# Window attention on one core: softmax tiles off ScalarE with one squaring instead of two, and a part of them finished by GpSimd alone

## The chip, the core and the metric

The kernel runs on one core of a Trainium2 chip. The core has five engines that run side by side: TensorE (PE in the profile, with its weight loads as PEld), ScalarE (ACT), VectorE (DVE), GpSimd (POOL) and SyncE (SP, which here issues transfers). Matmuls write to PSUM, eight banks of 512 float32 columns in each of 128 partitions; everything else is held in SBUF. The metric is the device time of one launch in microseconds. A run of the kernel before is one of 1052.92, 1053.43 and 1056.92 us; the median is 1053.43 us.

## The reference, cut to what matters

The input is an image of 224 x 224 tokens with 96 channels. The channels are split in two halves of 48. On the first half attention runs inside horizontal strips of 8 x 224 tokens, on the second half inside vertical strips of 224 x 8 tokens; there are 28 strips of each kind, and each strip has 1792 tokens.

```python
qkv = einsum('bhwc,cd->bhwd', x, wqkv)            # 96 -> 288, bfloat16
q, k, v = qkv[..., :96], qkv[..., 96:192], qkv[..., 192:]
scale = 48 ** -0.5
# for each of 28 horizontal strips (channels 0..47) and 28 vertical ones (channels 48..95):
a = softmax(q_strip @ k_strip.T * scale, axis=-1)  # 1792 x 1792
o_strip = a @ v_strip
out = concat(o_horizontal, o_vertical) @ wo        # 96 -> 96
```

The heavy part is the softmax: 56 matrices of 1792 x 1792 exponentials.

## The kernel before, in words

**Pairs and tiles.** Two strips are worked on together as a pair, one in the upper and one in the lower half of the partitions where that is possible. There are 28 pairs (P = 0 to 27), horizontal ones first (0 to 13), vertical ones after (14 to 27). A pair's queries are cut into four chunks of 512, 512, 512 and 256 columns, its keys into 14 blocks of 128. A tile of scores is 128 keys by 512 queries for both strips of the pair, so 128 partitions x 1024 columns in two PSUM banks (in the last chunk two key blocks of 256 queries each). A pair has 49 tiles, the kernel 1372.

**A tile's way.** Scores come from four matmuls (eight in the last chunk) of K against Q. They are in units in which 128 is a factor of two of the exponential. Then the tile is turned into exponentials in bfloat16, in one of `NPT` buffers called `PT` in SBUF. Last, two matmuls per key block multiply it with V and add it up in a PSUM bank (`pv_fn`, L692); a column of ones in V gives the softmax's denominator. When a chunk's tiles are all added up, DVE copies the bank to `OT_sb` (L1151), the output projection runs (L528, L563), and DVE divides by the denominator. For vertical strips the result is added to that of the horizontal ones, either on DVE (L590) or, after a DVE step into `tmp` (L577), on POOL (L581), and written out in pieces of 24 KB.

**Two kinds of tile.** The exponentials are made in two ways, and a table says for each pair and chunk how many tiles go the second way.

- On ScalarE (1128 tiles, kind "A"): one ACTIVATE with Exp over 128 x 1024, from PSUM into `PT` (L884). It takes no bias; its scale is ln2/128.
- Off ScalarE (244 tiles, kind "P"): the scores are computed with one more row, so that a constant of 17920 = 140 x 128 is added to them, which puts a float32 score's exponent at a fixed place: its upper 16 bits are the score cut down to a multiple of 128, its lower 16 bits the rest. PE computes the tile once into PSUM banks 6 and 7 ("s1", L679). DVE reads the lower halves, scales and shifts them and writes float32 into a buffer `qb` (called p1, L1174). POOL squares `qb` in place (L1100) and squares it again into `PT` as float16 (L1101). PE computes the same tile a second time ("s2", L679 too). DVE adds the upper halves, a constant and `PT`, and writes the sum as the 16 bits of the bfloat16 exponential into `PT` (called f, L1184).

The PSUM banks are shared out: 0 to 3 are two sets for ScalarE's tiles, 4 and 5 take the sums over V, and 4 to 7 are a ring for all else, where the pair 6 and 7 serves the tiles off ScalarE and can be a third set for ScalarE.

**What sets the order.** The program is planned when it is built. A planner (class `Sched` and the functions `step_pe`, `step_dve`, `step_pool`) goes through the work with fixed durations and latencies for each operation (constants at the file's head) and picks for each engine what comes next; the result is one straight list per engine. The table `HOW` has a row for each pair: three digits, how many tiles of each of the first three chunks go off ScalarE; a number that shapes when the next pair's projections come; and four groups of digits, which are the planner's thresholds in each chunk. Engines wait for each other by semaphores that count finished instructions; `settle` leaves out a wait that is already implied by another. On POOL every operation on a tile off ScalarE waits for the one before it on the same tile by POOL's own semaphore. POOL takes from its queue the piece of the earliest tile that is ready.

**Buffers.** A tile holds one of the 18 `PT` buffers from its first step to its product with V, and a tile off ScalarE holds one of the 5 `qb` buffers from p1 until POOL's last step.

The lines that the change touches are L17 to L68 (constants and `HOW`), L279 and L280 (constants of the extra row), L308 and L884 (the two kinds of Exp), L555 to L590 (the projection of the vertical strips), L1096 to L1110 (POOL's steps), L1149 (the copy's planned duration), L1173 to L1187 (p1 and f) and L1252 (the order of waits).

Of the kernel before, what the change touches and what calls it, by code (L numbers as in the profile page):

```python
# [24 lines left out]
SW_AB, SW_BA = SWT["AB"], SWT["BA"]  # L25
D_ACT, P_ACT, M_ACT, SEMA = 0.904, 0.9155, 1.0175, 0.053
D_MM, L_MM, L_PV, L_FILL = 0.216, 0.465, 0.44, 0.215
W_PE, W_FIN = 0.021, 0.08
SEMD, SEMP, SELF, SEMX = 0.15, 0.10, 0.19, 0.05
D_P1, D_SQ, D_ADD = 1.135, 1.9, 0.0019  # L30

# [8 lines left out]
HOW = [  # L40
    ("222", 4, "47621910043 47621610043 48111500102 48111500052"),
    ("433", 8, "31911900232 31911900133 31921900333 34921900333"),
    ("343", 12, "34922910333 21211710344 25211710344 25211710341"),
    ("234", 0, "25211710141 38512811234 38512811203 38911811203"),
    ("253", 8, "38912811203 22842702142 20913800234 38522510103"),
    ("131", 4, "38532510103 41242400243 29341900013 29641900113"),
    ("424", 6, "29641900141 29643900104 35141900263 35143700263"),
    ("332", 5, "35143710213 31831600124 31831600024 25711910144"),
    ("333", 12, "39912600343 39912600344 39912700244 56931812314"),
    ("344", 1, "36941812314 36911812312 22941910281 22941910171"),  # L50
    ("322", 12, "54342701072 4a631600103 4a532600102 4a542600202"),
    ("432", 9, "44542600202 44442600303 54442600203 44941700233"),
    ("435", 6, "54941700233 56513710273 33923700372 53913700372"),
    ("125", 6, "20411310241 20411510241 20411510243 36413510243"),
    ("332", 9, "5a121712204 5a121712004 5a121700004 55841800091"),
    ("332", 11, "55841800191 55841801394 55841801294 55841701294"),
    ("233", 12, "34222711191 28133400114 28233800112 28233800114"),
    ("243", 9, "28933800114 28932800194 58932802294 58932802194"),
    ("422", 9, "58942802394 42642700090 23341711232 23443711232"),
    ("233", 11, "23443711232 25441711234 25441711244 25441711244"),  # L60
    ("334", 3, "25441711204 25341711234 25341710232 25343710231"),
    ("333", 7, "2a343910234 56812810121 49431900323 34641710054"),
    ("233", 3, "34641710254 26921901034 26941901094 26941901034"),
    ("224", 3, "26931901034 29911901014 37121810224 33121810324"),
    ("333", 1, "33141810324 30131810124 30131800124 30131800124"),
    ("343", 7, "50131810124 50131610224 50111610224 26431810222"),
    ("233", 4, "24421810222 24421500222 24921501022 39632900141"),
    ("333", 7, "55542710102 25542700102 30132711054 33531400391"),  # L68
]
# [91 lines left out]
def bass_standalone__window_attn_cswin__vision_kernel(  # L161
# [27 lines left out]
    with es:  # L189
# [13 lines left out]
        one_sb = sb("one_sb", [1, 8], BF16)  # L203
        scr = sb("scr", [128, 8], FP32)
        warm = sb("warm", [128, 512], BF16)
        xs_sb = sb("xs_sb", [C, 2, 4], BF16)
# [71 lines left out]

        KC = [4.8125 / 128.0, 21.0]  # L279
        QC = [0.0, 32.0]  # L280

# [133 lines left out]
        def prep_fills(P):  # L415
# [3 lines left out]
            for kind, L in (("k", K), ("q", Q)):  # L419
                for c in range(NCH):  # L420
# [14 lines left out]
                    if kind == "k":  # L435
                        def d(e, bk, c=c, q0=q0, qs=qs):
                            return e.tensor_scalar(KT_sb[b][:, q0:q0 + qs], bk[:, 0:qs], alpha, None,  # L437
                                                   ALU.mult, ALU.add, accum_out=ksum[b][:, c:c + 1])
                        chain = [(0.07 + qs * 0.001026, d, [], [("KT", b, c), ("ksum", b, c)], None)]
                        rd = ["w0z", "w"]  # L440
                        needs = [("X", P)] if P else []
                        if P >= 2:
                            needs = needs + [("PV", P - 2)]
                        L.append(fill("B", 0.216 * qs / 512, pe_fn,
                                      rd + [("xT", b, 0), ("xT", b, 1)], chain, needs, ("K", P, c)))
                    else:
                        def d(e, bk, q0=q0, qs=qs):
                            return e.tensor_copy(QT_sb[b][:, q0:q0 + qs], bk[:, 0:qs])  # L448
# [3 lines left out]
                        L.append(fill("B", 0.216 * qs / 512, pe_fn,  # L452
                                      [("xT", b, 0), ("xT", b, 1), ("wqz", ph, b), ("wqc", ph, b),
                                       ("wq", ph, b, 0), ("wq", ph, b, 1)],
                                      [(0.07 + qs * 0.001026, d, [], [("QT", b, c)], da)],
                                      [("QB", P)], ("Q", P, c)))

# [9 lines left out]
            QB = fill("B", 0.36, pe_fn, [("wqT", ph)] + [("ksum", b, c) for c in range(NCH)],  # L467
                      [(0.08, d, [("wqz", ph, b)], [("wqc", ph, b)], None)],
                      [("K", P, c) for c in range(NCH)] + [("wqT", ph)], ("QB", P))
            for k0 in range(0, 2 * NKT, VS):  # L470
# [12 lines left out]
                def d(e, bk, k0=k0, n=n):  # L483
# [3 lines left out]
                V.append(fill("B", 0.033 * n, pe_fn, ["w"] + [("xT", b, w) for w in ws],  # L487
                              [(0.065 + n * 0.05, d, ["vones"], [("V", b, k0)], None)],
                              [("X", P)] if P else [], ("V", P, k0)))
# [21 lines left out]
        def fin_fills(P, fs):  # L511
# [98 lines left out]
        def dve_commit(item, t):  # L610
# [7 lines left out]
            after = 0.07 if k == 0 and f["gives"][0] == "fin" else 0.0  # L618
            S.commit("dve", t, st[0], st[0] + SEMD + after, lambda e, fn=st[1], bk=bk: fn(e, bk),
# [256 lines left out]
        def issue_qka(t, s):  # L876
# [7 lines left out]
            S.commit("act", 0.0, D_ACT, None, lambda e, s=s, slot=slot: e.activation(  # L884
                PT[slot][:], ps[:, 512 * SETS[s]:512 * SETS[s] + 1024], ACTF.Exp, scale=LN2 / 128.0),
                set_keys(s), pt_keys(slot), fresh=pt_keys(slot))
# [208 lines left out]
        def mids(tl):  # L1095
# [3 lines left out]
            qk, yk = [("q", i), "pser"], pt_keys(tl["slot"])  # L1099
            return [("pool", D_SQ, lambda e: e.tensor_tensor(q, q, q, ALU.mult), qk, [("q", i)]),  # L1100
                    ("pool", D_SQ, lambda e: e.tensor_tensor(y, q, q, ALU.mult), qk, yk)]  # L1101

        def next_mid(tl):
# [21 lines left out]
        def step_dve():  # L1125
# [20 lines left out]
            if what == "ot":  # L1146
                P, c = it["pc"]
                q0, qs = CH_Q0[c], CH_SIZES[c]
                d = 0.07 + qs * 0.001026  # L1149
                pb = pv_bank[it["pc"]]  # L1150
# [21 lines left out]
            elif what == "p1":  # L1172
                tl = it["t"]  # L1173
                S.commit("dve", t, D_P1, D_P1 + SEMD, lambda e: e.tensor_scalar(  # L1174
                    qb[tl["qb"]][:], half(U16, 0), QS * 2.0 ** -16, QS * QH, ALU.mult, ALU.add),
# [5 lines left out]
            elif what == "f":  # L1181
                tl = it["t"]
                ptk = pt_keys(tl["slot"])
                S.commit("dve", t, D_P1, D_P1 + SEMD, lambda e: e.scalar_tensor_tensor(  # L1184
                    PT[tl["slot"]][:].bitcast(U16), half(BF16, 1), 128.0 * (126.0 - SOFF + QC0),
                    PT[tl["slot"]][:].bitcast(FP16), ALU.add, ALU.add),
# [48 lines left out]
        def settle():  # L1235
# [88 lines left out]
```

## Time and profile before

| | |
|---|---|
| median of 3 runs | 1053.43 us (1052.92 to 1056.92) |
| the profiled execution | 1052.86 us, of which the profile's span is 1051.1 us |
| granted TensorE clock | 0.999 |
| ScalarE busy | 1040.3 us, 99% of the span |
| TensorE busy | 1029.0 us, 98% |
| GpSimd busy | 970.6 us, 92% |
| VectorE busy | 957.3 us, 91% |

How to read it. Busy is the time in which at least one instruction of the engine was running. A group of instructions is one source line, one engine and one form; after it stand the count, the busy time, the mean duration of one, and how long the engine stood idle just before such instructions. Successive ScalarE instructions overlap in the records (1128 of them with a mean of 1084 ns take 1036.0 us, not 1222.8), so the mean of one is longer than the time from start to start, and the time from start to start is what counts in a sum. The same holds, with a smaller overlap, for DVE and POOL. PE's busy time is modelled and is no proof that PE works at its best. The chain of work is followed back from the last instruction to what released it, step by step.

### The profile page before, as it was taken

The page shows a single profiled execution, that of the slowest core. Times are in us where ns is not written, and L with a number is a line of the kernel's source. Part 1 is how long each engine was busy: PE and PEld are TensorE (multiplying, and loading weights), DVE is VectorE, ACT ScalarE, POOL GpSimd, SP SyncE. Part 2 cuts the span into 40 slices and gives each one's busy share as a digit, 9 for nine tenths or more (in the row PEclk, how much of TensorE's full clock was granted, in tenths as well). Part 3 has the DMA queues.
Part 4 walks back from the last instruction along what each step waited for, and adds up shares of the span by engine and source line. Part 5 has one row for each costly group of instructions (what it writes and reads, how often), then busy time and mean ns, then how long its engine had stood idle before and what let it go on. Part 6 is the DMA issues. An engine that isn't in the chain of part 4 may idle for free.

```text
span 1051.1 us, 32414 instructions
## 1 busy us (share of the span) xinstructions
PE 1029.0 (98%) x14143; PEld 421.9 (40%) x14143; DVE 957.3 (91%) x1536; ACT 1040.3 (99%) x1139; POOL 970.6 (92%) x564
## 2 busy tenths in 40 slices
PE   8999999999999999999999999999999999999997
PEld 4433444444344344434434434434343343444333
DVE  7999999989989998999998899988999999999897
ACT  8999999999999999999999999999999999999997
POOL 6999899889989997998999999999999999999995
PEclk9999999999999999999999999999999999999999
DMA  4212113212220321111012212222213221321111
GB/s 101 64 42 63 30 48 63 54 32 56 64 55 11 76 41 46 42 37 37 2 36 46 43 39 56 52 36 49 51 23 55 56 50 23 55 55 24 24 21 34
DMA packets 162880, 47.12 MB, mean 45 GB/s; under 512 B 155895, under 2 KB 162711, under 8 KB 162738
## 3 DMA queue, kind: packets, MB, share of 16 engines
q1 hardware_dynamic: 161618, 44.57, 20.2%
q8 instruction: 110, 1.80, 0.7%
q10 hardware_dynamic: 1120, 0.49, 0.2%
q14 instruction: 32, 0.26, 0.1%
HBM read 10.60 MB, written 19.28 MB: 28 GB/s over the span
## 4 chain that ended last, share of the span: by engine, by line
ACT 96%; PE 2%; DVE 1%; issue 0%; DVEq 0%
ACT PT L884 96%; PE ps L666 1%; PE ps L692 1%; PE ps L343 0%; DVE PT L1184 0%; DVE qb L1174 0%; ACT xT_sb L743 0%; PE ps L679 0%; DVE out_all L590 0%; PE ps L432 0%; DVE QT_sb L448 0%; DVE OT_sb L1151 0%; PE ps L727 0%; PE ps L528 0%; PE ps L479 0%
## 5 line engine op out<-in xcount | busy, mean ns | idle before, releaser
L884 ACT ACTIVATE PT<-ps 128x1024 bf16<-128x1024 f32 x1128 | 1036.0, 1084 | 1.4 <-PE ps L666 1.2
L1100 POOL TENSOR_TENSOR qb<-qb 128x1024 f32<-128x1024 f32 x244 | 462.3, 1895 | 38.5 <-DVE qb L1174 36.6
L1101 POOL TENSOR_TENSOR PT<-qb 128x1024 f16<-128x1024 f32 x244 | 462.3, 1895 | 17.6
L666 PE MATMUL ps<-QT_sb,KT_sb 49*64 49x512 bf16 (+1 forms) x5296 | 462.9, 364 | 14.5 <-ACT PT L884 3.0
L692 PE MATMUL ps<-PT,V_sb 128*49 128x512 bf16 (+1 forms) x3136 | 464.5, 361 | 0.2 <-ACT PT L884 0.2
L1184 DVE SCALAR_TENSOR_TENSOR PT<-ps,PT 128x1024 uint16<-128x1024 bf16 x244 | 298.4, 1223 | 37.1 <-PE ps L679 27.9
L1174 DVE TENSOR_SCALAR qb<-ps 128x1024 f32<-128x1024 uint16 x244 | 298.0, 1221 | 19.4 <-PE ps L679 17.5
L666 PEld LDWEIGHTS ps<-QT_sb,KT_sb 49*64 49x64 bf16 x5296 | 134.4, 103 | 333.9 <-ACT PT L884 305.9
L692 PEld LDWEIGHTS ps<-PT,V_sb 128*49 128x49 bf16 x3136 | 137.4, 103 | 186.8 <-issue 153.3
L679 PE MATMUL ps<-QT_sb,KT_sb 50*64 50x512 bf16 x1952 | 194.0, 387 | 1.9 <-DVE PT L1184 0.3
L1151 DVE CAST OT_sb<-ps 113x512 bf16<-113x512 f32 x112 | 69.4, 620 | 8.8 <-PE ps L692 8.0
L679 PEld LDWEIGHTS ps<-QT_sb,KT_sb 50*64 50x64 bf16 x1952 | 55.6, 103 | 50.1 <-DVE qb L1174 11.9
L448 DVE CAST QT_sb<-ps 128x512 bf16<-128x512 f32 (+1 forms) x111 | 68.1, 616 | 5.6 <-PE ps L432 5.2
L437 DVE TENSOR_SCALAR_CACHE_REDUCE KT_sb<-ps 128x512 bf16<-128x512 f32 x108 | 66.0, 615 | 0.6 <-PE ps L432 0.4
L581 POOL TENSOR_TENSOR out_all<-tmp,Ph_sb 128x480 bf16<-128x480 f32 (+1 forms) x49 | 51.2, 1049 | 8.3 <-DVE tmp L577 7.9
L486 DVE CAST V_sb<-ps 128x480 bf16<-128x480 f32 (+1 forms) x84 | 52.1, 621 | 4.1 <-PE ps L479 3.4
L543 DVE TENSOR_TENSOR Ph_sb<-ps,rc 128x480 bf16<-128x480 f32 (+1 forms) x84 | 52.2, 622 | 2.5
L479 PEld LDWEIGHTS ps<-w_sb,xT_sb 96*64 96x64 bf16 x1568 | 36.0, 112 | 11.7 <-issue 5.8
L432 PE MATMUL ps<-xT_sb,wq_sb 97*64 97x512 bf16 x224 | 40.4, 360 | 0.0
L590 DVE SCALAR_TENSOR_TENSOR out_all<-ps,rc,Ph_sb 128x96 bf16<-128x96 f32 x160 | 39.2, 310 | 1.2
L432 PE MATMUL ps<-xT_sb,w_sb 97*64 97x512 bf16 x224 | 40.0, 359 | 0.0
L479 PE MATMUL ps<-w_sb,xT_sb 96*64 96x48 bf16 x1568 | 38.9, 190 | 0.0
(59 smaller groups left out, 274.5 us busy)
## 6 DMA issues: line engine op xcount, KB each, us to landing
cols_dram<-in_x_dram SPq DMA_DIRECT2D x28, 336.0 KB
out_dram<-out_all SPq DMA_DIRECT2D x386, 24.0 KB, 1.9
xT_sb<-cols_dram SPq DMA_TRANSPOSE x28, 4.5
xT_sb<-in_x_dram SPq DMA_TRANSPOSE x26, 4.2
xT_sb<-ones_dram SPq DMA_DIRECT2D x26, 7.0 KB
Ph_sb<-in_x_dram SPq DMA_DIRECT2D x2, 168.0 KB, 3.5
Ph_sb<-in_x_dram ACTq DMA_DIRECT2D x2, 168.0 KB, 3.7
out_dram<-out_all ACTq DMA_DIRECT2D x6, 24.0 KB, 1.9
```

The costliest lines, as they stand in the source:

```text
L432: ins = e.matmul(bk[64 * w:64 * w + 64, 0:qs], lhsT=lw, rhs=x_of(kind, w, q0, qs), start=True, stop=True)
L448: return e.tensor_copy(QT_sb[b][:, q0:q0 + qs], bk[:, 0:qs])
L479: ins = e.matmul(bk[64 * h:64 * h + 64, j * C2:(j + 1) * C2], lhsT=xT_sb[b][0:C, w, t0:t0 + 64], rhs=w_sb[0:C, wblk(P, "v"), 0:C2], start= ...
L666: ins = e.matmul(bank(SETS[s] + w)[64 * kh:64 * kh + 64, i * t["qs"]:(i + 1) * t["qs"]], lhsT=KT_sb[b][64 * w:64 * w + CA, kt * 128 + 64 * ...
L679: ins = e.matmul(bank(PB0 + w)[64 * kh:64 * kh + 64, 0:512], lhsT=KT_sb[b][64 * w:64 * w + nr, kt * 128 + 64 * kh:kt * 128 + 64 * kh + 64] ...
L692: ins = e.matmul(bank(pb)[64 * w:64 * w + CA, 0:t["qs"]], lhsT=V_sb[b][:, w, kt, :], rhs=PT[slot][:, ca:ca + t["qs"]], start=st and i == 0 ...
L884: S.commit("act", 0.0, D_ACT, None, lambda e, s=s, slot=slot: e.activation(PT[slot][:], ps[:, 512 * SETS[s]:512 * SETS[s] + 1024], ACTF.Ex ...
L1100: return [("pool", D_SQ, lambda e: e.tensor_tensor(q, q, q, ALU.mult), qk, [("q", i)]), ("pool", D_SQ, lambda e: e.tensor_tensor(y, q, q, ...
L1101: ("pool", D_SQ, lambda e: e.tensor_tensor(y, q, q, ALU.mult), qk, yk)]
L1151: S.commit("dve", t, d, d + SEMD, lambda e: e.tensor_copy(ot_dst(P, q0, qs), ot_src(P, pb, qs)), [("bank", pb)], [("OT", P % 2, c)], tag=( ...
L1174: S.commit("dve", t, D_P1, D_P1 + SEMD, lambda e: e.tensor_scalar(qb[tl["qb"]][:], half(U16, 0), QS * 2.0 ** -16, QS * QH, ALU.mult, ALU.add),
L1184: S.commit("dve", t, D_P1, D_P1 + SEMD, lambda e: e.scalar_tensor_tensor(PT[tl["slot"]][:].bitcast(U16), half(BF16, 1), 128.0 * (126.0 - S ...
```

## The change

- A tile off ScalarE needs one squaring instead of two. DVE's p1 scales the lower halves with other constants, POOL squares `qb` straight into `PT`, and f adds another constant.
- 275 tiles instead of 244 go off ScalarE; 1097 instead of 1128 stay on it.
- 118 of the 275 are "whole": p1 is a plain copy of the scores, float32 from PSUM to `qb`. POOL then does four steps alone: it scales and shifts the lower halves of `qb` into `PT` (float16), squares `PT` in place, scales and shifts it back into the lower halves of `qb` as 16-bit whole numbers, and converts `qb` to the 16 bits of the bfloat16 exponential in `PT`. Such a tile needs no second pass of scores and no f. The planner makes a tile whole when fewer tile steps are queued for POOL than a new, twelfth digit of `HOW` says. The other 157 go the way of before with one squaring less.
- The constants of the extra row change (21.75 and 31 for 21 and 32), so the added constant is no longer a multiple of 128. To give the same factor, ScalarE's Exp gets a bias: `up`, a [128, 1] operand in SBUF that DVE sets once at the start.
- `PT` has 16 buffers instead of 18, `qb` 6 instead of 5.
- In the last pair the projection comes in groups of 4 key blocks instead of 2, and all but the last group may be added on POOL; 60 additions are put on POOL instead of 49.
- `HOW` is another table, and several planned durations differ. Among waits of one DVE instruction, one for PE is considered first when waits that are implied are left out.

```diff
-QK, QH, QC0 = 0.00302015814, 3.83652076, 0.346271089
-QS = (128.0 * QK) ** 0.25
-SOFF = 140.0
+PA, PB, PS = 0.65763628, 0.33718946, 1.00172476
+QL, QQ = 128.0 * PA / PS, 128.0 * PB / PS
+QS, QH = QQ ** 0.5, 0.5 * QL / QQ
+SOFF = 580.0 * 31.0 / 128.0
-NPT = 18
-NQB = 5
+NPT = 16
+NQB = 6
-D_P1, D_SQ, D_ADD = 1.135, 1.9, 0.0019
+D_P1, D_SQ, D_ADD = 1.14, 1.852, 0.0019
+D_TS = 1.05
 HOW = [
-    ("222", 4, "47621910043 47621610043 48111500102 48111500052"),
+    ("211", 7, "217126001431 217126001434 386325000832 461239000223"),
...
-        KC = [4.8125 / 128.0, 21.0]
-        QC = [0.0, 32.0]
+        KC = [4.8125 / 128.0, 21.75]
+        QC = [0.0, 31.0]
...
-        now("act", ["scr"], ["scr2"], lambda e: e.activation(scr[:], scr[:], ACTF.Exp), dur=1.4)
+        dve_now(["up"], lambda e: e.memset(up[:], (SOFF - 127.0) * LN2 - math.log(PS)), 0.08)
+        now("act", ["scr", "up"], ["scr2"], lambda e: e.activation(scr[:], scr[:], ACTF.Exp, bias=up[:, 0:1]), dur=1.4)
...
+                        late = P == NP - 1 and k0 + n == NKT
-                        if P < NP - 1:
+                        if not late:
...
             S.commit("act", 0.0, D_ACT, None, lambda e, s=s, slot=slot: e.activation(
-                PT[slot][:], ps[:, 512 * SETS[s]:512 * SETS[s] + 1024], ACTF.Exp, scale=LN2 / 128.0),
+                PT[slot][:], ps[:, 512 * SETS[s]:512 * SETS[s] + 1024], ACTF.Exp, bias=up[:, 0:1], scale=LN2 / 128.0),
...
-                    for need, f in fin_fills(P, 2 if P == NP - 1 else FS):
+                    for need, f in fin_fills(P, 4 if P == NP - 1 else FS):
...
             qk, yk = [("q", i), "pser"], pt_keys(tl["slot"])
-            return [("pool", D_SQ, lambda e: e.tensor_tensor(q, q, q, ALU.mult), qk, [("q", i)]),
-                    ("pool", D_SQ, lambda e: e.tensor_tensor(y, q, q, ALU.mult), qk, yk)]
+            if not tl["whole"]:
+                return [("pool", D_SQ, lambda e: e.tensor_tensor(y, q, q, ALU.mult), qk, yk)]
+            lo = q.bitcast(U16).rearrange("p (n t) -> p n t", t=2)[:, :, 0]
+            bits = PT[tl["slot"]][:].bitcast(U16)
+            return [("pool", D_TS, lambda e: e.tensor_scalar(y, lo, 2.0 ** -16, QH, ALU.mult, ALU.add), qk, yk),
+                    ("pool", D_SQ, lambda e: e.tensor_tensor(y, y, y, ALU.mult), yk + ["pser"], yk),
+                    ("pool", D_TS, lambda e: e.tensor_scalar(lo, y, 512.0 * QQ, -512.0 * QQ * QH * QH, ALU.mult, ALU.add), yk + ["pser"], [("q", i)]),
+                    ("pool", D_TS, lambda e: e.tensor_scalar(bits, q, 1.0, 0.0, ALU.mult, ALU.add), qk, yk)]
...
                 qb_free.append(tl["qb"])
+                if tl["whole"]:
+                    pv_ready[(tl["P"], tl["c"])].append((tl, tl["slot"]))
+                    return
...
-                S.commit("dve", t, D_P1, D_P1 + SEMD, lambda e: e.tensor_scalar(
+                tl["whole"] = sum(m["what"] == "mid" for m in pool_q) < how()[11]
+                S.commit("dve", t, D_P1, D_P1 + SEMD, lambda e: e.tensor_copy(
+                    qb[tl["qb"]][:], ps[:, PB0 * 512:(PB0 + 2) * 512]) if tl["whole"] else e.tensor_scalar(
                     qb[tl["qb"]][:], half(U16, 0), QS * 2.0 ** -16, QS * QH, ALU.mult, ALU.add),
...
-                    PT[tl["slot"]][:].bitcast(U16), half(BF16, 1), 128.0 * (126.0 - SOFF + QC0),
+                    PT[tl["slot"]][:].bitcast(U16), half(BF16, 1), -QQ * QH * QH,
                     PT[tl["slot"]][:].bitcast(FP16), ALU.add, ALU.add),
...
-                        for s, v in sorted((x for x in waits if x[1]), key=lambda x: (-S.done[x], x)):
+                        for s, v in sorted((x for x in waits if x[1]), key=lambda x: (not (k == "dve" and x[0] == "pe"), -S.done[x], x)):
```

More of the change, by code (lines that the diff above doesn't have):

```diff
@@ L1 @@
+import math
 from contextlib import ExitStack
@@ L49 @@
[L49 to L64, printed above, removed]
@@ new lines @@
+    ("523", 12, "392317001614 5a8225000402 488329000443 264418102934"),
+    ("444", 10, "264419102934 264419102934 264419100934 264419101933"),
+    ("334", 4, "264319101933 267319001933 367319002933 364429002933"),
+    ("234", 10, "321429002933 321429002934 321129002934 587416000033"),
+    ("333", 12, "248128100543 411438002134 4a2419113401 564417102341"),
+    ("464", 0, "564417102343 325338113240 325338113244 383128101811"),
+    ("312", 10, "349128101811 349128101812 341228101812 355128103524"),
@@ new lines @@
+    ("343", 8, "355128103522 215438100222 215428100222 2a5428100224"),
+    ("353", 7, "219138001434 279138001431 453427100024 453437000024"),
+    ("323", 12, "453437000004 354417120014 354417123014 3a4427123010"),
+    ("444", 4, "3a4427123012 244118102010 557319012933 5a8317120012"),
+    ("424", 4, "5a8317122032 5a8317022332 5a8317122332 5a8317122331"),
+    ("335", 9, "5a8317122321 4a8317122424 4a8327022424 581427101532"),
+    ("413", 10, "582227101531 299116102414 484427010830 284427010830"),
@@ new lines @@
+    ("433", 6, "382327002044 382127002842 592426111342 292426101342"),
+    ("333", 11, "296419101342 286419101342 316429101123 316439101133"),
+    ("334", 8, "341417123821 341417122821 341427122021 373429100712"),
+    ("444", 4, "576417121542 5a6417021543 5a6417002543 5a6417002243"),
+    ("323", 6, "5a6336122322 5a6336122322 4a6326122320 495225112221"),
+    ("423", 12, "495325012221 229428102632 229428102631 5a6426100122"),
+    ("434", 1, "5a6429103122 577336020343 577336020341 547336020343"),
@@ L438, in d @@
                                                    ALU.mult, ALU.add, accum_out=ksum[b][:, c:c + 1])
-                        chain = [(0.07 + qs * 0.001026, d, [], [("KT", b, c), ("ksum", b, c)], None)]
+                        chain = [(0.08 + qs * 0.001026, d, [], [("KT", b, c), ("ksum", b, c)], None)]
                         rd = ["w0z", "w"]
@@ L466, in d @@
                                        mybir.AxisListType.X, ALU.add)
-            QB = fill("B", 0.36, pe_fn, [("wqT", ph)] + [("ksum", b, c) for c in range(NCH)],
+            QB = fill("B", 0.43, pe_fn, [("wqT", ph)] + [("ksum", b, c) for c in range(NCH)],
                       [(0.08, d, [("wqz", ph, b)], [("wqc", ph, b)], None)],
@@ L487, in prep_fills @@
                 V.append(fill("B", 0.033 * n, pe_fn, ["w"] + [("xT", b, w) for w in ws],
-                              [(0.065 + n * 0.05, d, ["vones"], [("V", b, k0)], None)],
+                              [(0.075 + n * 0.05, d, ["vones"], [("V", b, k0)], None)],
                               [("X", P)] if P else [], ("V", P, k0)))
@@ L617, in dve_commit @@
                 more = [("tmp", st[6]["ti"][0])]
-            after = 0.07 if k == 0 and f["gives"][0] == "fin" else 0.0
+            after = -0.06 if k == 0 and f["gives"][0] == "fin" else 0.0
             S.commit("dve", t, st[0], st[0] + SEMD + after, lambda e, fn=st[1], bk=bk: fn(e, bk),
```

28 lines of the change are left out of this document (12 added, 16 removed).

## The prediction

> **What bounds the kernel now.** I read the page first (busy time, the chain that ended last, the costliest groups), then the chain in order of time, then POOL's timeline, its groups by shape and the load by stretches of time.
>
> ```profile
> span 1051.1 us, 32414 instructions
> PE 1029.0 (98%) x14143; PEld 421.9 (40%) x14143; DVE 957.3 (91%) x1536; ACT 1040.3 (99%) x1139; POOL 970.6 (92%) x564
> ...
> ACT 96%; PE 2%; DVE 1%; issue 0%; DVEq 0%
> ...
> L884 ACT ACTIVATE PT<-ps 128x1024 bf16<-128x1024 f32 x1128 | 1036.0, 1084 | 1.4 <-PE ps L666 1.2
> L1100 POOL TENSOR_TENSOR qb<-qb 128x1024 f32<-128x1024 f32 x244 | 462.3, 1895 | 38.5 <-DVE qb L1174 36.6
> L1101 POOL TENSOR_TENSOR PT<-qb 128x1024 f16<-128x1024 f32 x244 | 462.3, 1895 | 17.6
> ...
> L1184 DVE SCALAR_TENSOR_TENSOR PT<-ps,PT 128x1024 uint16<-128x1024 bf16 x244 | 298.4, 1223 | 37.1 <-PE ps L679 27.9
> L1174 DVE TENSOR_SCALAR qb<-ps 128x1024 f32<-128x1024 uint16 x244 | 298.0, 1221 | 19.4 <-PE ps L679 17.5
> ...
> L679 PE MATMUL ps<-QT_sb,KT_sb 50*64 50x512 bf16 x1952 | 194.0, 387 | 1.9 <-DVE PT L1184 0.3
> ...
> L581 POOL TENSOR_TENSOR out_all<-tmp,Ph_sb 128x480 bf16<-128x480 f32 (+1 forms) x49 | 51.2, 1049 | 8.3 <-DVE tmp L577 7.9
> ```
>
> The chain is 96% the Exp of L884, and that group stood idle for 1.4 us in all: ScalarE is the bound from its first tile to its last. The chain in order of time shows the pace and both ends:
>
> ```profile
> 9.14 58.88 ACT PT L884 x64
> ...
> 213.31 604.34 ACT PT L884 x658
> ...
> 1045.38 0.42 PE ps L692 x4
> ```
>
> 658 tiles take 604.34 us, 0.9185 us from start to start. Of the span, 9.1 us lie before the first tile, 1036 are tiles (1128 x 0.9185), some 6 us from 1045.38 on are the last tile's product with V, the projection and the write out. The profiled execution took 1052.86 us, 1.76 above the span, and 0.57 below the median of 1053.43.
>
> **The change part by part.**
>
> *Fewer tiles on ScalarE.* 1097 instead of 1128: 31 x 0.9185 = 28.5 us off the bound, if nothing else ends later. That is the gain to be had; the other parts decide whether it is kept.
>
> *POOL's load.* POOL is next to look at, because it takes on work of a new kind. Its rows by time and by shape:
>
> ```profile
> 14.07 1.89 POOL L1100 TENSOR_TENSOR qb<-qb 128x1024 f32<-128x1024 f32 x1 [3.82 <-DVE qb L1174]
> ...
> 503.43 1.90 POOL L1101 TENSOR_TENSOR PT<-qb 128x1024 f16<-128x1024 f32 x1
> 505.28 1.89 POOL L1100 TENSOR_TENSOR qb<-qb 128x1024 f32<-128x1024 f32 x1
> 507.25 1.89 POOL L1101 TENSOR_TENSOR PT<-qb 128x1024 f16<-128x1024 f32 x1
> ...
> 1037.34 1.89 POOL L1101 TENSOR_TENSOR PT<-qb 128x1024 f16<-128x1024 f32 x1
> ```
>
> ```profile
> L324 POOL COPY w_sb<-wst 96x192 bf16<-96x192 bf16 x1 | 0.3, 341 | 2.0 <-DMA wst<-in_wqkv_dram 2.0
> L316 POOL COPY wq_sb<-wst 96x96 bf16<-96x96 bf16 x4 | 1.1, 263 | 0.2
> L335 POOL MEMSET wqT<- 128x192 bf16 x2 | 0.5, 262 | 0.1
> L332 POOL MEMSET woh<- 128x97 bf16 x1 | 0.2, 188 | 0.1
> ```
>
> A squaring followed by work of another tile takes 1.85 us from start to start (503.43 to 505.28); followed by the next step of its own tile 1.97 (505.28 to 507.25), so a wait on POOL's own step costs 0.12. Before, POOL worked from 14.07 to 1039.23. Now the sum:
> - Squarings: 157 + 118 = 275 instead of 488, at 1.85: 509 us instead of 903. That the operands are float16 in 118 of them has no row; float16 out costs what float32 out costs (both 1895 ns), so I take the same.
> - New steps with one input (L1110, L1112, L1113 of the changed kernel): 3 x 118 = 354. None is in this trace. From below: the memsets' slope is (262 - 188) / 95 = 0.78 ns a column, which gives 188 + 927 x 0.78 = 911 ns for 1024 columns. From above: the two-input squaring, 1895 ns. Nearest is the copy, one input and one output: (341 - 263) / 96 = 0.81 ns a column, 341 + 832 x 0.81 = 1015 ns. I take 1.02: 361 us.
> - Additions: 60 instead of 49 at 1.05 (51.2 / 49): 63 us instead of 51.
> - Own waits: in the program's order 328 steps follow a step of their own tile directly, before 225: 39 us instead of 27.
>
> The total is 972 us instead of 981, in a span shorter by 28.5: 25 us spare of about 997. So POOL nearly fills its time, and the halves differ. Additions exist only for the vertical pairs:
>
> ```profile
> 20.00:540.00 520.00, 514.81 (x7088) 210.72 (x7084) 479.52 (x704) 519.88 (x567) 477.64 (x255) 1.00 0.20 47
> 540.00:1040.00 500.00, 489.88 (x6744) 198.27 (x6744) 457.90 (x774) 499.94 (x546) 481.13 (x280) 1.00 0.21 41
> ```
>
> (columns: stretch, its length, busy us of PE, PEld, DVE, ACT and POOL with counts, clock, transfer share, GB/s). In pairs 14 to 27 of the changed program stand 545 tiles on ScalarE, 500.6 us, and for POOL 141 squarings (260.9), 156 one-input steps (159.1), 60 additions (63.0) and 142 own waits (17.0): 500.0 us. In pairs 0 to 13 it is 507.0 against 472.2. So in the second half POOL has no time to spare and ScalarE will wait for it now and then: through `PT` buffers that come free late, since a chunk's sum waits for its last tile. I add 4 us for that; it is what 156 steps at 1.045 instead of 1.02 would cost. The bounds are 0, as in the trace (1.4 us idle), and, at the two-input price, 354 x 0.88 - 25 = 287 us.
>
> *DVE.* p1 275 times, f 157 times: 432 x 1.222 = 528 us instead of 596; the whole tiles' plain copy is taken at p1's price, same columns, same place read. 11 more additions move to `tmp` and POOL, and DVE's own final steps become fewer. DVE falls to some 890 us of 1023; nothing is late through it.
>
> *PE.* 275 + 157 = 432 passes of L679 instead of 488, 56 x 4 matmuls at 0.099 us (194.0 / 1952) = 22 us less, and 31 tiles of L666 less. PE's cover gets better, not worse. The clock is 1.00 in both stretches above, and PE stays about as full.
>
> *The bias.* Each of the 1097 Exp now reads `up`. Its setting is one DVE memset during the start, before ScalarE's wait for the first transposes; it costs nothing. Reading it has no row on ScalarE. Nearest are DVE's evacuations with and without a [128, 1] operand:
>
> ```profile
> L448 DVE CAST QT_sb<-ps 128x512 bf16<-128x512 f32 x83 | 56.7, 684 | 5.6 <-PE ps L432 5.2
> L448 DVE CAST QT_sb<-ps 128x256 bf16<-128x256 f32 x28 | 11.6, 414 | 0.0
> L760 DVE TENSOR_SCALAR KT_sb<-ps,kb_sb 128x512 bf16<-128x512 f32 x2 | 1.4, 748 | 1.0 <-PE ps L432 1.0
> L760 DVE TENSOR_SCALAR KT_sb<-ps,kb_sb 128x256 bf16<-128x256 f32 x1 | 0.5, 476 | 0.0
> ```
>
> With the operand one instruction is 62 ns longer at 256 columns (476 against 414) and 64 at 512. That is the mean of one, not the time from start to start. On ScalarE one instruction shows 1084 ns and the next starts after 918, so 166 ns of each lie under its neighbour, and a fetch of 62 ns has room there: the operand is constant, and the tile after next stands ready (1.4 us idle in 1128). I take 0, with 0.062 as the other end; that end is a rival below, because it would turn the sign. A gain is excluded: nothing is taken away from the instruction.
>
> *Buffers, queues, the end.* Two `PT` buffers fewer are weighed against a shorter hold: a tile with one squaring gives its `PT` up about 1.97 us sooner, 157 times; a whole one holds it about as long as before, 5.3 us of POOL steps (3 x 1.02 + 1.85 + 3 x 0.12) against 3.85 for two squarings and 1.22 for f. One more `qb` covers the whole tile's four steps. The rest of the price is in the 4 us. Transfers out stay 392; four of the last go from ACT's to SP's queue. SP issued 19 in 13.25 us at the end, 0.7 each:
>
> ```profile
> 1035.73 13.25 SPq L269 DMA_DIRECT2D out_dram<-out_all  x19
> 1044.97 4.33 ACTq L269 DMA_DIRECT2D out_dram<-out_all  x6
> ```
>
> Four more are 2.8 us at worst, nothing if they are issued before the last chunk is done, as the coarser groups of the last pair (4 blocks) make likely; no Exp stands behind those on ACT. I take 0. The changed order of DVE's waits takes no wait away; 0, bounded by DVE's idle time of 9%.
>
> *Sum.* 1052.86 - 28.5 + 4 = 1028.4 for an execution like the profiled one; with 0.57 for the median 1028.9. I say 1028.
>
> **The rivals.**
>
> *The bias is paid in full (slower).* If a fetch of 62 ns lies between two Exp, as the DVE rows would have it, ScalarE's pace is 0.980: 1028 + 1097 x 0.062 = 1096 us. The point from which it decides is 28.5 / 1097 = 0.026 us a tile. For it speaks that both widths give the same addition on DVE, so it is a fixed cost of the operand; against it the overlap of 166 ns. The Trainium skill (ScalarE: Activation LUTs, What ACT_TABLE_LOAD costs) states about 93 ns for each [128, 1] operand of an ACTIVATE; by that the sum would be 1028 + 1097 x 0.093 = 1130 us, an estimate from that page. No run so far shows an ACTIVATE with such an operand, so the trace neither agrees nor differs.
>
> *POOL becomes the bound (late, or slower).* Each 0.1 us on a one-input step adds 35 us to POOL. Up to 1.09 us (1.02 + 25 / 354) the whole still fits; at 1.17 the gain is gone; at 1.25 the time is about 972 + 81 + 26 (its start and the end after it) + 2 = 1081 us. What could do it: the lower halves are read and written two bytes of every four, and types are converted, which the copy's row does not show. In the mild case the second half's 156 steps set it, from 1024.4: 1034 is reached at 1.02 + 9.6 / 156 = 1.08, and 1048 at 1.17.
>
> *The change does nothing for the bound.* If the wait for POOL's longer tiles kept ScalarE from 28 us in all, the time would stay at 1053. No wait in the trace is near that size: all of ScalarE's idle time was 1.4 us.
>
> **How the numbers follow.** About 0.5% (5 us) is what a measurement of this kernel can tell from no change. ScalarE stays the bound and POOL just keeps up (1018 to 1034): 0.67. POOL late by some 6 to 20 us (1034 to 1048): 0.13. Below 1018: 0.01, only if ScalarE's pace itself gets better with less work on PE. No change: 0.02. POOL decidedly the bound (over 1059): 0.05. The bias paid (1075 to 1130): 0.12. So faster 0.81, same 0.02, slower 0.17. The range 1018 to 1047 is that of the first two cases, 0.80; the likeliest one's own is 1018 to 1034.
>
> **What would show it.** In the changed kernel's page: the Exp group x1097 with about 1007 us busy, 0.918 from start to start, and a few us of idle time before it; a start to start near 0.98 or 1.01 proves the bias. POOL's three one-input groups with a mean near 1.02 to 1.06; over 1.1 POOL is late, and then waits by PE for `PT` written on POOL appear and ScalarE's idle time grows, most of all after 540 us. L1107 and L1111 at 1.85 to 1.9. The chain still over 95% Exp. DVE near 890 us busy.

## The result, and the profile after

The changed kernel takes 1125.89 us (median of 4 runs, 1121.34 to 1129.87) against 1053.22 us for the kernel before on the same chip (4 runs): a ratio of 1.068, 95% interval 1.0626 to 1.0734. It is 6.8% slower. The forecast of 1028 us had the wrong sign. What came is the first rival, the bias paid in full.

The page of the changed kernel (profiled execution 1123.16 us; span, busy time, chain by engine, costliest groups):

```profile
span 1121.3 us, 31675 instructions
PE 1023.4 (91%) x13792; PEld 393.7 (35%) x13792; DVE 913.7 (81%) x1441; ACT 1106.7 (99%) x1108; POOL 985.8 (88%) x716
...
ACT 98%; PE 1%; DVE 0%; issue 0%; DVEq 0%
...
L890 ACT ACTIVATE PT<-ps,up 128x1024 bf16<-128x1024 f32 x1097 | 1102.3, 1356 | 2.5 <-PE ps L672 2.5
...
L1107 POOL TENSOR_TENSOR PT<-qb 128x1024 f16<-128x1024 f32 x157 | 294.0, 1893 | 4.8 <-DVE qb L1191 4.7
...
L1111 POOL TENSOR_TENSOR PT<-PT 128x1024 f16<-128x1024 f16 x118 | 223.3, 1892 | 9.2
...
L1110 POOL TENSOR_SCALAR PT<-qb 128x1024 f16<-128x1024 uint16 x118 | 123.2, 1044 | 62.6 <-DVE qb L1190 52.3
L685 PE MATMUL ps<-QT_sb,KT_sb 50*64 50x512 bf16 x1728 | 169.2, 380 | 1.5 <-ACT PT L890 1.4
L1112 POOL TENSOR_SCALAR qb<-PT 128x1024 uint16<-128x1024 f16 x118 | 158.6, 1344 | 10.3
L1190 DVE COPY qb<-ps 128x1024 f32<-128x1024 f32 x118 | 144.4, 1224 | 22.6 <-PE ps L685 19.6
L1113 POOL TENSOR_SCALAR PT<-qb 128x1024 uint16<-128x1024 f32 x118 | 123.2, 1044 | 9.7
```

ScalarE is still the bound, more than before: the chain is 98% Exp, and that group stood idle for 2.5 us in all. But 1097 Exp are now busy for 1102.3 us, where 1128 of them took 1036.0. That is 1.0048 us each against 0.9184. The chain in order of time says the same:

```profile
8.99 531.47 ACT PT L890 x529
...
548.03 564.62 ACT PT L890 x562
...
1112.69 0.42 PE ps L698 x4
```

529 tiles in 531.47 us are 1.0047 us each. In the trace's start times the distance from one Exp to the next that occurs most often, in half of all cases, went from 904 to 996 ns (the median from 905 to 996), so some 92 ns were added; in the mean, in which the longer distances of both kernels count too, it is 86 ns. The mean of one in the records went from 1084 to 1356 ns.

From these rows the whole difference of the two spans (70.2 us) comes out, term by term:

| | us |
|---|---|
| before the first Exp: 8.99 instead of 9.14 | -0.15 |
| 31 Exp fewer, at 0.9185 | -28.5 |
| 1097 Exp longer by 1.0048 - 0.9184 = 0.0864 | +94.8 |
| idle before Exp: 2.5 instead of 1.4 | +1.1 |
| after the last Exp: 1121.3 - 1112.69 = 8.6 instead of 5.7 | +2.9 |
| sum | +70.15 |

The chain shows one more thing, a stretch of 7.5 us between the two long pieces of Exp. The load by stretches around it (columns as in the prediction's table):

```profile
530.00:540.00 10.00, 9.09 (x116) 3.39 (x112) 6.20 (x15) 10.00 (x11) 9.50 (x8) 1.00 0.01 2
540.00:548.00 8.00, 7.62 (x88) 2.85 (x84) 5.61 (x7) 6.69 (x7) 7.66 (x6) 0.57 0.01 2
548.00:560.00 12.00, 11.51 (x150) 4.28 (x146) 10.34 (x14) 11.97 (x13) 11.74 (x8) 1.00 0.37 79
```

TensorE's granted clock was 0.57 in the mean of these 8 us and ScalarE lost 1.3 us. The clock was 0.995 over this execution, and went from 0.986 (1129.87 us) to 0.997 (1121.34 us) in the four runs.

### The profile page after: what moved, and what is told of

Same layout as the page of the kernel before. It is cut to its first block, busy times and chain, and to the rows that moved or that the text cites. A ratio compares the mean times of both kernels' runs of the same rounds, so it can differ in the third digit from the quotient of the medians.

```text
span 1121.3 us, 31675 instructions
## 1 busy us (share of the span) xinstructions
PE 1023.4 (91%) x13792; PEld 393.7 (35%) x13792; DVE 913.7 (81%) x1441; ACT 1106.7 (99%) x1108; POOL 985.8 (88%) x716
## 4 chain that ended last, share of the span: by engine, by line
ACT 98%; PE 1%; DVE 0%; issue 0%; DVEq 0%
ACT PT L890 98%; PE ps L348 0%; PE ps L672 0%; PE ps L698 0%; ACT xT_sb L749 0%; PE ps L733 0%; PE ps L484 0%; PE ps L685 0%; DVE out_all L596 0%; DVE xT_sb L745 0%; DVE OT_sb L1166 0%; PE ps L437 0%; PE ps L569 0%; DVE warm L310 0%; DVE rc L576 0%
## 5 line engine op out<-in xcount | busy, mean ns | idle before, releaser
L890 ACT ACTIVATE PT<-ps,up 128x1024 bf16<-128x1024 f32 x1097 | 1102.3, 1356 | 2.5 <-PE ps L672 2.5
L1107 POOL TENSOR_TENSOR PT<-qb 128x1024 f16<-128x1024 f32 x157 | 294.0, 1893 | 4.8 <-DVE qb L1191 4.7
L1191 DVE TENSOR_SCALAR qb<-ps 128x1024 f32<-128x1024 uint16 x157 | 192.2, 1224 | 48.8 <-PE ps L685 42.4
L1111 POOL TENSOR_TENSOR PT<-PT 128x1024 f16<-128x1024 f16 x118 | 223.3, 1892 | 9.2
L1201 DVE SCALAR_TENSOR_TENSOR PT<-ps,PT 128x1024 uint16<-128x1024 bf16 x157 | 192.1, 1224 | 38.4 <-PE ps L685 34.3
L1110 POOL TENSOR_SCALAR PT<-qb 128x1024 f16<-128x1024 uint16 x118 | 123.2, 1044 | 62.6 <-DVE qb L1190 52.3
L685 PE MATMUL ps<-QT_sb,KT_sb 50*64 50x512 bf16 x1728 | 169.2, 380 | 1.5 <-ACT PT L890 1.4
L1112 POOL TENSOR_SCALAR qb<-PT 128x1024 uint16<-128x1024 f16 x118 | 158.6, 1344 | 10.3
L1190 DVE COPY qb<-ps 128x1024 f32<-128x1024 f32 x118 | 144.4, 1224 | 22.6 <-PE ps L685 19.6
L1113 POOL TENSOR_SCALAR PT<-qb 128x1024 uint16<-128x1024 f32 x118 | 123.2, 1044 | 9.7
```

The lines of the kernel that those rows point to most:

```text
L685: ins = e.matmul(bank(PB0 + w)[64 * kh:64 * kh + 64, 0:512], lhsT=KT_sb[b][64 * w:64 * w + nr, kt * 128 + 64 * kh:kt * 128 + 64 * kh + 64] ...
L1107: return [("pool", D_SQ, lambda e: e.tensor_tensor(y, q, q, ALU.mult), qk, yk)]
L1110: return [("pool", D_TS, lambda e: e.tensor_scalar(y, lo, 2.0 ** -16, QH, ALU.mult, ALU.add), qk, yk), ("pool", D_SQ, lambda e: e.tensor_t ...
L1111: ("pool", D_SQ, lambda e: e.tensor_tensor(y, y, y, ALU.mult), yk + ["pser"], yk),
L1112: ("pool", D_TS, lambda e: e.tensor_scalar(lo, y, 512.0 * QQ, -512.0 * QQ * QH * QH, ALU.mult, ALU.add), yk + ["pser"], [("q", i)]),
L1113: ("pool", D_TS, lambda e: e.tensor_scalar(bits, q, 1.0, 0.0, ALU.mult, ALU.add), qk, yk)]
```

## The experiments

The theory after the result: the [128, 1] operand `up` costs some 90 ns in each Exp, and this is all of the loss. The rival: POOL is late too, since one of its new steps takes 1344 ns (the mean of one) where I had summed with 1020, and would hold the time up without the operand. Seven kernels were run.

**1. The same kernel, the bias as a constant.** Only the small Exp at the start, over 8 columns, still reads `up`.

```diff
-... ACTF.Exp, bias=up[:, 0:1], scale=LN2 / 128.0),
+... ACTF.Exp, bias=(SOFF - 127.0) * LN2 - math.log(PS), scale=LN2 / 128.0),
```

> The changed kernel with the Exp's bias given as a constant of the instruction (the same value, 9.334) and not as the [128, 1] operand; nothing else differs. Theory A, the operand's fetch: in the changed kernel's trace the tiles of ScalarE start 996 ns apart at the median, in the trace of before 904, so 92 ns each; here they should be 904 apart again, and the time should fall by 1097 x 0.092 = 101 us to about 1025, plus what POOL makes late: its steps L1110 and L1113 take 1.01 us from start to start and L1112 1.31, which puts POOL's load at 1004 us in a time of about 997, so I expect 1028 to 1045. Theory B, POOL or the new order is what made it slow and the Exp's spacing only follows: the time stays above 1090 and ScalarE shows idle time.

Measured: 1061.74 us (median of 10 runs, 1056.15 to 1068.46), ratio to the kernel before 1.0072 (1.0042 to 1.0102). The time is 64 us below that of the changed kernel, but 17 us above the upper end of what was expected, and even without the operand the change gains nothing. Page, waits (us in total, times, longest) and stretches of this kernel:

```profile
span 1065.3 us, 31675 instructions
PE 1021.3 (96%) x13792; PEld 411.3 (39%) x13792; DVE 893.0 (84%) x1441; ACT 1019.2 (96%) x1108; POOL 986.0 (93%) x716
...
POOL 62%; ACT 14%; PE 13%; DVE 7%; issue 3%; DVEq 0%; POOLq 0%
...
L890 ACT ACTIVATE PT<-ps 128x1024 bf16<-128x1024 f32 x1097 | 1014.8, 1074 | 33.7 <-PE ps L672 31.9
...
L1112 POOL TENSOR_SCALAR qb<-PT 128x1024 uint16<-128x1024 f16 x118 | 159.3, 1350 | 10.3
```

```profile
PEld ps L685 <- DVE PT L1201: 33.9, 74, 2.1
...
ACT PT L890 <- PE ps L672: 31.9, 48, 2.5
...
DVE PT L1201 <- POOL PT L1107: 26.1, 31, 2.9
```

```profile
640.00:650.00 10.00, 9.97 (x138) 4.08 (x136) 8.13 (x20) 10.00 (x12) 9.59 (x9) 1.00 0.28 58
650.00:660.00 10.00, 8.17 (x70) 2.49 (x70) 7.22 (x12) 6.96 (x8) 10.00 (x7) 0.68 0.43 84
660.00:670.00 10.00, 10.00 (x70) 2.58 (x64) 5.13 (x6) 6.93 (x7) 9.41 (x8) 0.50 0.14 27
```

The Exp is back at a median of 904 ns from start to start. The chain is now 62% POOL, and the waits show how a late POOL reaches ScalarE: f (L1201) waits for the squaring, PE waits for f before it can write banks 6 and 7 again, ScalarE waits for PE's scores. The last fence shows a second loss on top: POOL is busy for all of the 10 us from 650, PE pauses, the clock falls to half, and 20 us hold 15 Exp instead of some 22. Over the ten runs the time follows the clock: 1068.46 us at 0.974, 1056.15 at 0.990, 0.77 us for each 0.001. Drawn on to a full clock, which none of the ten had, that is about 1048 us. By this estimate some 20 of the 34 us above the forecast are POOL's lateness and some 13 the clock that falls after it; the split was not measured.

**2. The kernel before, with the operand (zeros) in its Exp.** The small Exp at the start reads it too.

```diff
+        dve_now(["up"], lambda e: e.memset(up[:], 0.0), 0.08)
-... ACTF.Exp, scale=LN2 / 128.0),
+... ACTF.Exp, bias=up[:, 0:1], scale=LN2 / 128.0),
```

> The kernel before with one edit: its Exp reads a [128, 1] bias in SBUF that holds zeros; same tiles, same order. Theory A: 1128 x 0.092 = 104 us more, 1157 us (1150 to 1165), Exp 996 ns apart. Theory B (the operand costs nothing in a row of Exps): 1053 us as before. A price between, as of DVE's 62 ns, would give 1123.

Measured: 1153.49 us (1152.18 to 1156.63), ratio 1.0941 (1.0912 to 1.097): 99.9 us more, 89 ns for each of 1128 tiles, and within what was expected. The tiles and the order are those of the kernel before, so the operand's price doesn't come from the new order or from POOL.

```profile
span 1154.5 us, 32415 instructions
...
L886 ACT ACTIVATE PT<-ps,up 128x1024 bf16<-128x1024 f32 x1128 | 1135.0, 1347 | 5.6 <-PE ps L668 5.6
```

**3. Constant bias, no whole tiles.** This asks what the 118 tiles done by POOL alone are worth.

```diff
-                tl["whole"] = sum(m["what"] == "mid" for m in pool_q) < how()[11]
+                tl["whole"] = False
```

> As the first of these runs (constant bias), and no tile is whole: all 275 tiles off ScalarE go through p1, one squaring and f. This tells what the whole tiles are worth. DVE then has 550 steps of 1.224 us, 673 us, beside about 385 us of other work (913.7 less 192.2, 192.1 and 144.4): 1058 us. Theory: DVE becomes the bound, 1065 to 1085 us, POOL falls to some 600 us busy. Rival: one squaring alone is what helps, and the whole tiles only load POOL: at or below the first run's time.

Measured: 1217.6 us, ratio 1.1531 (1.1479 to 1.1582), far above what was expected, and not for the reason given: DVE is busy for 1018.5 us of 1226.3, POOL for 606.6, no engine is full, and TensorE's granted clock was 0.901.

```profile
PE 1144.1 (93%) x14277; PEld 442.6 (36%) x14277; DVE 1018.5 (83%) x1476; ACT 1030.1 (84%) x1108; POOL 606.6 (49%) x385
...
L890 ACT ACTIVATE PT<-ps 128x1024 bf16<-128x1024 f32 x1097 | 1025.7, 1063 | 171.6 <-PE ps L672 169.8
```

ScalarE waits for 171.6 us. The table `HOW` was made for a plan with whole tiles, and that its order doesn't fit without them is the likely reason, but no run shows it. What whole tiles are worth under an order of their own stays open.

**4. The changed kernel, planned with the Exp's real duration.**

```diff
-D_ACT, P_ACT, M_ACT, SEMA = 0.904, 0.9167, 1.0175, 0.053
+D_ACT, P_ACT, M_ACT, SEMA = 0.996, 1.006, 1.1095, 0.053
```

> The changed kernel with its operand, and the planner's three constants for an Exp raised by 0.092 us (0.996, 1.006, 1.1095), so that the order fits the true pace. It tells how much of the loss is the operand itself and how much a plan that did not know it. Theory A: 1097 x 1.005 + 17 = 1120 us; the few us of low TensorE clock (0.57 of full speed from 540 to 548 us in the changed kernel's trace) go, because the planner puts filling matmuls into PE's longer pauses; 1115 to 1123 and a smaller spread. Rival: the plan was the larger part: below 1090.

Measured: 1195.58 us, ratio 1.1334 (1.1308 to 1.136). It missed both expectations.

```profile
L890 ACT ACTIVATE PT<-ps,up 128x1024 bf16<-128x1024 f32 x1097 | 1111.5, 1157 | 56.2 <-PE ps L672 55.5
```

The Exp group stood idle for 56.2 us (2.5 in the changed kernel) and the clock was 0.953. The likely reason, as in the third run, is that the thresholds in `HOW` don't fit durations they weren't made for. The new order hides what was asked: how much of the loss a plan that knows the operand could win back stays open.

**5. Constant bias, and POOL's dear step made dense.** L1112 writes 16-bit numbers into the lower halves of `qb`, so two bytes of every four. Here it writes the same numbers side by side into a buffer of its own; no other step is moved. The last step still reads `qb`, so this kernel leaves the correction that L1112 makes out of the whole tiles: their exponentials are only roughly right, and the run prices the step but isn't a version to use. (The bias line is that of the first run; the lines of this kernel are numbered one higher.)

```diff
+        s16 = [sb(f"s16_{i}", [128, 1024], U16) for i in range(NQB)]
-... lambda e: e.tensor_scalar(lo, y, 512.0 * QQ, ...
+... lambda e: e.tensor_scalar(s16[i][:], y, 512.0 * QQ, ...
```

> The changed kernel with the constant bias of the first run, same order, and one more edit: POOL's step L1112 writes its 1024 numbers of 16 bits next to each other into a buffer of its own, not into the lower halves of the 32-bit words of qb (two bytes of every four). The correction it computes is thereby left out of the whole tiles' result, so their exponentials are only roughly right; every instruction, its size and its place in the order stay. In the run with the constant bias L1112 took 1350 ns where L1110, which reads two bytes of every four, and L1113, which reads and writes densely, took 1047 each. Theory A, the write with gaps is what POOL was short by: L1112 goes to 1045 ns, POOL's load falls by 118 x 0.3 = 36 us, ScalarE's 34 us of idle time goes below 10, the chain is Exp again, and the time falls from 1061.7 to 1024 to 1034 us, the forecast's value without the operand. Theory B, its float16 input or its conversion is what costs, or the order is what makes ScalarE wait: L1112 stays at 1.35 us, or the time stays above 1050.

Measured: 1029.47 us (1026.95 to 1032.85), ratio 0.978 (0.9745 to 0.9815), within what was expected. Page, and POOL's groups by shape:

```profile
span 1025.4 us, 31675 instructions
PE 998.8 (97%) x13792; PEld 408.6 (40%) x13792; DVE 891.3 (87%) x1441; ACT 1011.7 (99%) x1108; POOL 950.7 (93%) x716
...
ACT 92%; PE 3%; POOL 2%; DVE 1%; issue 0%; DVEq 0%
...
L891 ACT ACTIVATE PT<-ps 128x1024 bf16<-128x1024 f32 x1097 | 1007.4, 1089 | 1.3 <-PE ps L673 1.2
```

```profile
L1114 POOL TENSOR_SCALAR PT<-qb 128x1024 uint16<-128x1024 f32 x118 | 123.6, 1047 | 9.7
L1111 POOL TENSOR_SCALAR PT<-qb 128x1024 f16<-128x1024 uint16 x118 | 123.6, 1047 | 28.9 <-DVE qb L1191 19.7 <-DVE wq_sb L471 0.5
L1113 POOL TENSOR_SCALAR s<-PT 128x1024 uint16<-128x1024 f16 x118 | 123.6, 1047 | 10.3
```

The step (now L1113) falls from 1350 to 1047 ns, the price of the other two, and the time falls by 32.3 us (1061.74 - 1029.47) where POOL's work falls by 118 x 0.303 = 35.8 us. So the gaps in the write cost 0.3 us a step, and reading with the same gaps (L1111) costs nothing. This kernel stands where the forecast stood: some 1028 us is the time of the change without the operand and with each one-input step near the price I had taken. That it comes so close is in part luck: the 4 us forecast for ScalarE's waits did not come, and 3 us at the end, which I had taken at 0, did.

**6. The changed kernel, operand kept, with the dense write.**

> The changed kernel with its bias operand, and only L1112 writing densely into a buffer of its own (the correction is left out of the whole tiles' result, as in the run before). It tells what POOL's dear step costs while the operand is there. Theory A, the operand alone bounds the changed kernel and covers POOL: ScalarE's pace of 1.005 us a tile gives POOL 1103 us for 1004 us of work; 1118 to 1126 us, no change beyond 0.5%. Rival, the two add up: 1125.9 - 32 = 1094.

Measured: 1127.51 us (1121.81 to 1130.67), ratio 1.0686 (1.064 to 1.0731), the same as the changed kernel and 1.5 us above the upper end of what was expected.

```profile
L891 ACT ACTIVATE PT<-ps,up 128x1024 bf16<-128x1024 f32 x1097 | 1104.3, 1351 | 7.5 <-PE ps L673 7.5
```

The 36 us of POOL work that it saves are worth nothing while ScalarE takes 1.007 us a tile (1104.3 / 1097).

**7. Constant bias, new order.** The constant as in the first run, the dear step planned at 1.305 us and the other two at 1.01, and a new `HOW` made for that (not shown): 259 tiles off ScalarE, 113 of them whole. Everything is computed as in the changed kernel.

```diff
-D_TS = 1.05
+D_TS, D_TS2 = 1.01, 1.305
```

> A version meant to beat both: the changed kernel with the constant bias, planned with POOL's steps at their measured prices (1.01 us for L1110 and L1113, 1.305 for L1112) and with a table of its own: 259 tiles off ScalarE, 113 of them whole, 1113 on it. Everything is computed. If the two causes found are all there is: 1113 x 0.9185 + 15 + 1.8 = 1039 us, 1036 to 1046, ScalarE idle for less than 5 us. POOL's load is 259 x 1.85 + 113 x 3.33 + 61 x 1.03 + 40 = 958 of some 1010 us. Rival, a third cause in the scheme with whole tiles: above 1050.

Measured: 1054.25 us (median of 10 runs, 1048.24 to 1057.84), ratio 0.9989 (0.9964 to 1.0013): no difference from the kernel before, and 8 us above the upper end of what was expected. By the words of the expectation this is its rival, a third cause beside the operand and the dear step.

```profile
PE 1006.3 (96%) x13749; PEld 404.2 (38%) x13749; DVE 861.9 (82%) x1408; ACT 1029.6 (98%) x1124; POOL 938.8 (89%) x686
...
ACT 53%; POOL 32%; PE 8%; DVE 4%; issue 2%; DVEq 0%; POOLq 0%
...
L890 ACT ACTIVATE PT<-ps 128x1024 bf16<-128x1024 f32 x1113 | 1025.1, 1092 | 10.4 <-PE ps L672 9.1
```

In the profiled execution (1054.49 us, a clock of 0.989) ScalarE was idle for 10.4 us where less than 5 was expected, POOL still stands in a third of the chain, and the ten runs spread from 1048.24 us at a clock of 0.998 to 1057.84 at 0.985. Lateness that this order leaves, and the clock, are what the rows show; which of them comes first, and whether another order would remove it, stays open. No version that computes everything and is clearly faster than the kernel before was found.

## Why the prediction was wrong

**The step that failed** is the bias: "I take 0, with 0.062 as the other end". Its argument was that 166 ns of each Exp lie under its neighbour in the records, and that a fetch has room there. The second run shows that it has none: the kernel before with nothing but the operand added is 99.9 us slower. The records show why the argument was no argument. The mean of one grew by 272 ns (1084 to 1356) while the starts moved apart by 92, so the overlap itself grew, from 180 to 360 ns. In the fourth run, with the same operand and again 996 ns from start to start, the mean of one is 1157 ns and the overlap 161. So the overlap says nothing of the price: time shown twice in two records isn't a gap in which the engine was free. With 1.4 us of idle time in 1128 tiles ScalarE was full, and the addition came on top.

What spoke for the price was in the prediction: the DVE rows, with 62 and 64 ns, nearly the same at both widths. The measured price is 92 ns from start to start, 89 ns a tile in the second run, and 91 ns in the record of the one small Exp over 8 columns at the start:

```profile
L308 ACT ACTIVATE scr<-scr 128x8 f32<-128x8 f32 x1 | 0.2, 209 | 0.0
L313 ACT ACTIVATE scr<-scr,up 128x8 f32<-128x8 f32 x1 | 0.3, 300 | 0.0
```

The first row is the kernel before, the second the changed one. So at 8 and at 1024 columns it is the same fixed cost. The Trainium skill (ScalarE: Activation LUTs, What ACT_TABLE_LOAD costs) gives about 93 ns for each [128, 1] operand of an ACTIVATE; the runs agree with that figure, and the rival's 1130 us by it lies 4 us above the 1125.89 measured. By the DVE rows the rival gave 1096 us. Its chance of 0.12 was too low: the same addition in two DVE rows stood against one reading of an overlap, and the sign turned at 0.026 us a tile, less than half of 0.062.

**The term that was mis-sized** is POOL's one-input step. I took 1.02 us for all three. L1110 and L1113 have it (1044 ns the mean of one, 1.01 from start to start); L1112, which writes with gaps, takes 1.31 (1.43 to the next step of its tile, less the 0.12 of the wait). So POOL's sum was 118 x 0.29 = 34 us short, more than the 25 us I had called spare. With the operand this is hidden (the sixth run); without it, it costs 32 us, more than the whole gain of 24 us that the fifth run has over the kernel before (the first run against the fifth). The rival "POOL becomes the bound" named this doubt, the two bytes of every four, but put it on reads and writes alike. At the mean of the three steps, 1.11 us, its working gives 1024.4 + 156 x 0.09 = 1038 us; the first run measured 1061.74. Two things are missing in that working. By its sum the first half still fits (472.2 + 198 x 0.09 = 490 of 507.0 us), yet half of the first run's waits of ScalarE for scores, 15.7 of 31.9 us, lie before 540 us: a sum over a half doesn't show where POOL is late for a while. And the clock that falls after such a wait is not in it.

**Point by point, the rest:**

- 31 tiles fewer: right. In the fifth run 1097 Exp are busy for 1007.4 us, 0.918 each, as forecast.
- Squarings: right. 1893 ns, and 1892 with float16 in, where no row had stood.
- The 4 us for ScalarE's waits, and the buffers: too much. In the fifth run, with 16 `PT` and 6 `qb`, ScalarE's idle time before Exp is 1.3 us; it was 1.4 in the kernel before.
- DVE: right, 891.3 us in the fifth run against 890 (913.7 in the changed kernel, with the same instructions); the plain copy costs p1's 1224 ns.
- PE: the second passes fell by 24.8 us (194.0 to 169.2; 22 forecast). "PE stays about as full", with a clock of 1.00, was wrong for the changed kernel, 91% at 0.995; in the fifth run it is 97%, at 0.998 in the profiled execution and 0.991 to 0.998 in all four.
- The end: 2.9 us longer, where I took 0 with 2.8 as the bound. The fifth run has it too (1025.4 - 1016.61 = 8.8 us, below), so it belongs to the change and not to the operand. The traces say where it comes from: SP's queue.

The chain of the fifth run, its last Exp and the first step of the end:

```profile
875.17 141.40 ACT PT L891 x154
1016.61 0.42 PE ps L699 x4
```

The transfers out at the end of the changed kernel:

```profile
1009.58 109.93 SPq L273 DMA_DIRECT2D out_dram<-out_all  x95
1114.71 1.29 ACTq L273 DMA_DIRECT2D out_dram<-out_all  x2
```

SP issues until 1119.51 us, 6.8 us after the start of the step behind the last Exp (1112.69). In the kernel before SP was done 3.6 us after that start (1048.98) and ACT, with six, 3.9 us (1049.30). The span ends 1.8 us after the last issue in both. DVE's last step comes no later than before: 2.4 us after that start (1115.13), where it was 2.9 (1048.26). So what lengthens the end is the four transfers that moved from ACT's queue to SP's, and it costs about the 2.8 us that the prediction gave as its bound. No run puts them back.

- The setting of `up` at the start: right, the first Exp starts at 8.99 instead of 9.14 us. The order of DVE's waits has no run of its own.

## What to carry to other kernels

On an engine that is the bound from end to end, count each fixed addition to its instruction in full, times the instructions: a constant in place of the operand was worth 64 us here (1125.89 against 1061.74), and 98 us where nothing else stood in the way (1127.51 against 1029.47). Overlap between records is no spare time; idle time is. And a step that is new on an engine should be priced with its access pattern, on the side it writes as well as on the side it reads, before a plan is fitted to it: this plan was fitted to 1.05 us for a step that takes 1.31.

## What the runs showed of the hardware that I had not expected

- A [128, 1] bias costs an ACTIVATE some 92 ns although the operand never changes: 91 in the record of one at 8 columns, 92 from start to start at 1024, back to back.
- POOL's one-input step over 1024 columns takes 1044 ns when it reads two bytes of every four, and 1344 when it writes so; 1047 when it writes densely.
- TensorE's granted clock falls to half for some microseconds without any long pause of PE before. In the changed kernel's trace it is 0.50 for 6.8 us from 540.4 us on, and the pauses in the 5 us before are at most 0.38 us:

```profile
537.49 0.41 PE L672 MATMUL ps<-QT_sb,KT_sb 49*64 49x512 bf16 x4 [0.30 <-ACT PT L890]
...
538.49 0.41 PE L672 MATMUL ps<-QT_sb,KT_sb 49*64 49x512 bf16 x4 [0.38 <-ACT PT L890]
...
539.50 0.41 PE L672 MATMUL ps<-QT_sb,KT_sb 49*64 49x512 bf16 x4
...
540.50 0.64 PE L672 MATMUL ps<-QT_sb,KT_sb 49*64 49x512 bf16 x4 [0.38 <-ACT PT L890]
```

These are rows of PE's timeline (start, length, count, idle time before). The same four matmuls take 0.41 us until 539.5 and 0.64 from 540.5 on. What sets off the fall is not settled by these runs. In the first run's trace five such falls, of 3.4 to 17.1 us, each begin within 5 us of a pause of 0.86 to 1.83 us, yet other pauses of that size, such as 1.17 us at 203.7, are followed by none. The kernel before shows it too: beside the first run it took 1056.9 to 1057.3 us at a mean clock of 0.994 to 0.995 and 1052.5 to 1054.4 at 0.999 to 1.
